# Windowed attention into a gated feed-forward block: token blocks cut 256 x4 and 512 x4, and the work of attention groups 3, 4 and 5 set at other places

## The chip, the cores and the metric

The kernel runs as one program on one core of a Trainium2 chip. The metric is the time of one execution on the device in microseconds (us), and lower is better. A core has five engines with instruction queues of their own: TensorE (PE in the profile, with its weight loads as PEld), VectorE (DVE), ScalarE (ACT), GpSimd (POOL) and SyncE (SP). They meet only through semaphores. DMAs are issued from the queues of POOL, SP and ACT; those from POOL are the profile's software queue q0, those from SP and ACT its hardware queues q1 and q10.

## The reference

```
# q, k, v: (4, 8, 768, 64) f32; n_sink = 4, window = 128
s = q @ k.T / 8
keep = (j < n_sink) or (0 <= i - j < window)       # query i, key j
a = softmax(where(keep, s, -1e9))
x = (a @ v) with the heads side by side            # 3072 tokens x 512
out = (silu(x @ w_gate) * (x @ w_val)) @ w_out     # 512 -> 1536 -> 512
```

Tokens run batch by batch: token 768*b + i is position i of batch b.

## The kernel before

**Groups and blocks.** Attention works in 12 groups of 256 tokens, three for each batch: group g is part g % 3 of batch g // 3. The feed-forward works in eight blocks of tokens, listed in `SIZES` (L42), with `OFF` as their starts. Before, block 3 is groups 3 and 4, block 4 is 5 and 6, block 5 is 7 and 8, block 6 is 9 and 10, and block 7 is group 11 alone. All matmuls are in bf16 with sums in f32.

**The steps of a group.**
- `load_nat` (L106): four POOL DMAs bring k and q of 256 tokens with tokens on partitions (the tile `nat`). From group 4 on there is one buffer for it, so the next load waits until the last has been turned. `load_v` (L143) brings the values, for the later groups of a batch (`load_vm`, L120) by three or five smaller DMAs into the tile `vm`, else by two into `va`.
- Turning k and q so that the head dimension lies on partitions (tiles `kT`, `qT`). Two ways are there: `step_TN` (L273) with 4 TensorE transposes for each of four quarters and a copy out of PSUM, or `xbar` (L287) with four DMA transposes from the queue of SP, which is called the crossbar here.
- Scores: `step_S1` (L360) issues the matmuls of all heads into six PSUM banks of the eight, `exps` the exponentials on ACT, `masks` the masking on DVE; `step_S2` and `step_S3` are the later exponentials and masks. Groups that are not the first of a batch also have the sinks' scores, `mm_K` (L422).
- Values: `step_PV` (L469), four calls for each group, with a reciprocal and a scaling on DVE that make the tile `xn`.
- `step_X` (L523): from group 3 on, one DMA transpose from SP for each 128 tokens writes `xn` into the block's `xT`, which the feed-forward reads.

**The steps of a block.** `gate` (L611) is one unit: matmuls with w_gate into `pg`, the tanh on ACT, matmuls with w_val into `pv`, two operations of DVE that write `ht`. A block of 512 tokens has 12 such units of 4 + 4 matmuls with 512 columns; a block of 256 has 6 units of 8 + 8 matmuls with 256 columns. `down` (L644) is one unit for each 128 tokens: 12 matmuls, a copy on ACT, and a DMA to the output from the queue of ACT for the early blocks and of SP for the others (L665).

**The order.** It is written out by hand. `weave` (L714) walks through a list of gate and down units and hands to unit i the attention steps that `slots` (L719) names for i. In a gate the steps lie between the two halves of the matmuls, or ahead of both where they are marked so (as `S1` is). In a down they are spread evenly over its 12 matmuls. `one(at, g)` (L687) puts the scores of g at unit `at` and the last masks one later; `pair(ga, gb)` (L873) puts two groups into a weave of 16 units.

The first weave has, before, 24 units: 0 to 11 are the gates of blocks 0 and 1, 12 to 17 the gates of block 2, 18 to 23 the downs of blocks 0, 1 and 2. In it lie groups 2, 3 and 4. Each of the next three weaves has 16 units, the 12 gates and 4 downs of a block of 512, with two groups of the next block. The last has the gates of blocks 6 and 7 and then their downs, with group 11. In block 3 the first gate is done in two halves of 256 columns (`(3, i)`), so that the second half of its tokens may arrive later.

**What orders the loads.** All loads are in one POOL queue, in program order. `behind(tb, t)` (L701) is a one-element copy on POOL that reads token t of a block's `xT`: POOL stands there until that DMA transpose has landed, and the loads after it start later. `turned(g)` (L705) does the same for `qT`. The transposes of a group by the crossbar, those of `xn` and the later output DMAs share the SP queue, again in program order. A DMA from SP or ACT takes one of eight semaphores in turn, and waits until the DMA that had it last has landed.

Of the kernel before, what the change touches and what calls it, by code (L numbers as in the profile page):

```python
# [14 lines left out]
def kernel(  # L15
# [12 lines left out]
    nc = tc.nc  # L28
    P = 128
# [9 lines left out]
    NP2 = H // 2  # L39
    GC = S // 256  # L40
    NG = B * GC
    SIZES = [256, 256, 256, 512, 512, 512, 512, 256]  # L42
    assert sum(SIZES) == NTOK and NG == 12
    OFF = [sum(SIZES[:i]) for i in range(len(SIZES))]
    PEX = (0, 1, 2)
# [34 lines left out]
    def bank(shape, dtype, name):  # L80
        return psum.tile(shape, dtype, tag="b", name=name)
# [97 lines left out]
    vcl = const.tile([P, B - 1, D + 1], FP32)  # L179
# [4 lines left out]
    one = const.tile([P, 1], FP32)  # L184
# [56 lines left out]
    def flush():  # L241
        firsts()
        for f in later:
            f()
        later.clear()
# [274 lines left out]
    def dense(t, c, n):  # L520
        return t[:, 0:c * n].rearrange("p (c n) -> p c n", c=c)

    def step_X(g, j, evict="v"):  # L523
        t0 = g * 256 + j * P
        tb = max(i for i in range(len(SIZES)) if OFF[i] <= t0)
        off = t0 - OFF[tb]
        if tb == 0 and off == 0:
            xTs["01"] = xtp.tile([P, DMC, 512], BF16, tag="xT", name="xT")
            xTs[0], xTs[1] = (xTs["01"][:, :, 256 * i:256 * (i + 1)] for i in range(2))
        elif tb > 1 and off == 0:  # L530
            xTs[tb] = dense(xtp.tile([P, DMC * 512], BF16, tag="xT", name="xT"),
                            DMC, SIZES[tb])
            if tb == 3:
                for i in range(2):
                    xTs[tb, i] = xTs[tb][:, :, 256 * i:256 * (i + 1)]
        if g not in PEX:
            def sp():
                nc.sync.dma_start_transpose(xTs[tb][:, :, off:off + P], xns[g, j])
            later.append(sp)
            return  # L540
        pt = bank([P, DMC, P], BF16, "px")
        for i in range(DMC):
            nc.tensor.transpose(pt[:, i], xns[g, j][:, i * P:(i + 1) * P], ident)  # L543

        if evict == "a":
            nc.scalar.copy(out=xTs[tb][:, :, off:off + P], in_=pt)
            return

        def dve():
            nc.vector.tensor_copy(out=xTs[tb][:, :, off:off + P], in_=pt)  # L550
        if evict == "now":
            dve()
        else:
            later.append(dve)
# [18 lines left out]
    def new_h(tb):  # L573
        if tb not in hts:
            n = SIZES[tb]
            t = hpool.tile([P, DFC * 512], BF16, tag="ht", name="ht")
# [13 lines left out]
    def gate_v(tb, f, pg, th, pv):  # L590
# [11 lines left out]
        if tb == "01":  # L602
# [4 lines left out]
        nc.vector.tensor_tensor(  # L607
            hts[tb][:, f:f + 512 // SIZES[tb]].rearrange("p a n -> p (a n)"), u, pv,
            op=ALU.mult)
# [23 lines left out]
    def gate_first(tb, f, attn):  # L633

        step_PV(1, 0, 1, "a")
        step_PV(1, 1, 1)
        flush()
        a = gate_a(tb, f)
        step_X(1, 1, "now")
        step_X(1, 0, "a")  # L640
        held.pop()()
        gate_b(tb, f, *a)

    def down(tb, ts, attn, last=False):  # L644
        at = {}
        for i, a in enumerate(attn):
            at.setdefault(DFC * (i + 1) // (len(attn) + 1), []).append(a)
        n = DFC // 4
        r0 = OFF[tb] + ts * P
        parts = [(0, 3 * P), (3 * P, DM)] if last else [(0, DM)]  # L650
        for m, (lo, hi) in enumerate(parts):
            po = bank([P, hi - lo], FP32, "pd")
            for f in range(DFC):
                for a in at.get(f, []) if m == 0 else []:
                    a()
                    flush()
                nc.tensor.matmul(  # L657
                    po, hts[tb][:, f, ts * P:(ts + 1) * P], wos[f // n][:, f % n, lo:hi],
                    start=(f == 0), stop=(f == DFC - 1))
            ot = opool.tile([P, hi - lo], FP32, tag=f"ot{hi - lo}", name="ot")  # L660
            if m == 0:
                nc.scalar.activation(ot, po, AF.Copy, scale=0.5)  # L662
            else:
                nc.vector.tensor_scalar(ot, po, 0.5, None, op0=ALU.mult)  # L664
            (nc.scalar if tb < 3 else nc.sync).dma_start(out[r0:r0 + P, lo:hi], ot)  # L665

    def gates(tb):
        return [(gate, tb, f) for f in range(0, DFC, 512 // SIZES[tb])]

    def downs(tb):  # L670
        return [(down, tb, t) for t in range(SIZES[tb] // P)]

    def A(fn, *a):
        return lambda: fn(*a)

    def TN(g, evict="av"):
        return [A(step_TN, g, i, j, evict) for j in range(2) for i in range(2)]
# [4 lines left out]
    def S1(g, apart=False):  # L682
        f = A(step_S1, g, apart)
        f.ahead = True
        return f

    def one(at, g, apart=False):  # L687
        return [(at, [S1(g, apart), A(step_S2, g, apart)]), (at + 1, [A(step_S3, g)])]

    def ahead(f):  # L690
        g = lambda: f()
        g.ahead = True
        return g

    def PVs(g):
        return [A(step_PV, g, j, hh) for hh in range(2) for j in range(2)]

    def Xs(g):
        return [A(step_X, g, j) for j in range(2)]
# [14 lines left out]
    def weave(us, slots):  # L714
        assert all(i < len(us) for i in slots)
        for i, (fn, tb, x) in enumerate(us):
            fn(tb, x, slots.get(i, []))

    def slots(*pairs):  # L719
        sl = {}  # L720
        for at, steps in pairs:
            for i, step in zip(at if isinstance(at, tuple) else (at,) * len(steps),
                               steps):
                sl.setdefault(i, []).append(step)
        return sl
# [117 lines left out]
    for f in masks1[:3]:  # L843
        f()

    g0, g1, g2 = gates(0), gates(1), gates(2)
    us = [(gate_held, *g0[0][1:]), (gate_first, *g0[1][1:]), g1[0], g1[1],
          *((gate, "01", f) for f in range(4, DFC)),
          *g2, *downs(0), *downs(1), *downs(2)]

    def L(*fs):
        def f():
            for x in fs:
                x()
        return f

    def NV(g):
        return L(A(load_nat, g), A(load_v, g))
# [2 lines left out]
        (4, TN(2)[::2]), (5, TN(2)[1::2]), ((6, 7), Ss(2)), (6, [K(2)]),  # L861
        ((8, 8), PVs(2)[:2]), (9, [A(step_PV, 2, 0, 1, "a"), A(step_PV, 2, 1, 1, "a")]),
        ((10, 11), [A(step_X, 2, 0, "a"), ahead(A(step_X, 2, 1, "a"))]),
        (11, [NV(4), lambda: nc.gpsimd.tensor_copy(out=vcl[64:128], in_=vcl[0:64])]),
        ((14, 14, 15, 15), TN(3, "aa")),
        (15, [A(xbar, 4)]), (15, [A(load_nat, 5)]), (19, [A(xbar, 5, (0,))]),
        *one(17, 3), (18, [A(step_ks, 1)]), (18, [A(step_vsb, 1)]),
        ((19, 19, 19, 20), PVs(3)), (19, [S1(4)]), (20, [L(A(step_S2, 4), A(step_S3, 4))]), (20, Xs(3)), (20, [A(xbar, 5, (1,))]),
        ((21, 21, 21, 22), PVs(4)), (21, Xs(4)[:1]),
        (22, [Xs(4)[1], flush, A(behind, 3, 511), A(load_v, 5), A(load_nat, 6)]),  # L870
        (23, [A(xbar, 6), A(turned, 6), A(load_v, 6), NV(7)])))

    def pair(ga, gb, at=0):  # L873
        return [*one(at, ga), ((4, 4, 5, 5), PVs(ga)), ((7, 7), Xs(ga)), *one(8, gb, True),
                ((12, 12, 13, 13), PVs(gb)), ((13, 13), Xs(gb))]

    weave([(gate, (3, i), 0) for i in range(2)] + gates(3)[2:] + downs(3), slots(
        (15, [A(step_ks, 2), A(step_vsb, 2)]), *pair(5, 6), (9, [flush, A(xbar, 7)]),
        (13, [flush, A(behind, 4, 511), NV(8)]),
        (15, [A(xbar, 8)]), (15, [NV(9)])))  # L880
    weave(gates(4) + downs(4), slots(
        *pair(7, 8), (3, [A(xbar, 9)]), (15, [A(step_ks, 3), A(step_vsb, 3)]),
        (3, [A(load_nat, 10)]), (13, [flush, A(behind, 5, 511), A(load_v, 10), NV(11)]),
        (15, [A(xbar, 10)])))
    weave(gates(5) + downs(5), slots(*pair(9, 10), (6, [A(xbar, 11)])))
    us = gates(6) + gates(7) + downs(6) + downs(7)
    us[-1] = (lambda tb, t, a: down(tb, t, a, True), *us[-1][1:])
    weave(us, slots(
        *one(0, 11), ((4, 4, 5, 5), PVs(11)), ((8, 9), Xs(11))))


# [33 lines left out]
```

## Time and profile before

| what | value |
|---|---|
| median of 3 runs | 234.45 us (233.47 to 234.68) |
| the profiled execution: its time, its span | 233.82 us, 231.9 us |
| granted TensorE clock, mean over the span | 0.993 |
| PE busy | 225.6 us, 97% of the span |
| DVE, ACT, POOL busy | 150.9, 106.4, 84.3 us |
| software DMA queue q0 | 79904 packets, 80.7% of 16 engines' span |
| hardware DMA queue q1 | 30672 packets, 26.7% |
| chain that ended last | PE 94% of the span |

The span runs from the first instruction to the last; the 1.9 us beside it lie outside the instructions. A matmul's end is modelled, so that a row of matmuls begins a little before the previous one's shown end; the step from one start to the next is the time that it took. A DMA share over 1 means that packets of several DMAs are open at once on an engine.

### The profile page before, as it was taken

The page shows a single profiled execution, that of the slowest core. Times are in us where ns is not written, and L with a number is a line of the kernel's source. Part 1 is how long each engine was busy: PE and PEld are TensorE (multiplying, and loading weights), DVE is VectorE, ACT ScalarE, POOL GpSimd, SP SyncE. Part 2 cuts the span into 40 slices and gives each one's busy share as a digit, 9 for nine tenths or more (in the row PEclk, how much of TensorE's full clock was granted, in tenths as well). Part 3 has the DMA queues.
Part 4 walks back from the last instruction along what each step waited for, and adds up shares of the span by engine and source line. Part 5 has one row for each costly group of instructions (what it writes and reads, how often), then busy time and mean ns, then how long its engine had stood idle before and what let it go on. Part 6 is the DMA issues. An engine that isn't in the chain of part 4 may idle for free.

```text
span 231.9 us, 5433 instructions
## 1 busy us (share of the span) xinstructions
PE 225.6 (97%) x2155; PEld 125.4 (54%) x2155; DVE 150.9 (65%) x327; ACT 106.4 (46%) x212; POOL 84.3 (36%) x123
## 2 busy tenths in 40 slices
PE   7699999999999999999999999999999999999994
PEld 3469645796555644455444454454454544487443
DVE  5878888767660797960797970597960599778000
ACT  4784486566543726423635512835612823333221
POOL 8996874960500907806353415135000000000000
PEclk9979999999999999999999999999999999999999
DMA  8999999999998998998989996989915102000132
GB/s 147 150 185 179 179 198 206 164 156 122 123 154 230 103 134 99 151 195 141 146 119 139 128 124 138 105 109 144 117 40 144 45 3 42 3 3 0 64 120 90
DMA packets 112008, 28.04 MB, mean 121 GB/s; under 512 B 99056, under 2 KB 109040, under 8 KB 111984
## 3 DMA queue, kind: packets, MB, share of 16 engines
q0 software_dynamic: 79904, 14.29, 80.7%
q1 hardware_dynamic: 30672, 11.58, 26.7%
q10 hardware_dynamic: 1408, 1.84, 2.5%
q8 instruction: 17, 0.28, 0.5%
q14 instruction: 7, 0.06, 0.1%
HBM read 29.13 MB, written 6.29 MB: 153 GB/s over the span
## 4 chain that ended last, share of the span: by engine, by line
PE 94%; DMA 2%; POOL 2%; DVE 0%; issue 0%; POOLq 0%
PE pg L564 27%; PE pv L564 27%; PE pd L657 27%; PE o L494 4%; PE s L382 3%; DMA rows<-in_q_dram 2%; PE s L326 1%; PE o L463 1%; PE pk L432 1%; PE pn L279 1%; PE o L454 1%; POOL rows L102 1%; POOL x L216 1%; PE px L543 1%; DVE xT L550 0%
## 5 line engine op out<-in xcount | busy, mean ns | idle before, releaser
L592 DVE SCALAR_TENSOR_TENSOR u<-th,pg 128x512 bf16<-128x512 f32 x72 | 49.2, 683 | 45.4 <-ACT th L584 45.1
L564 PE MATMUL pg<-xT,wg 128*128 128x512 bf16 (+1 forms) x360 | 74.2, 337 | 0.3 <-DVE xT L550 0.3
L564 PE MATMUL pv<-xT,wv 128*128 128x512 bf16 (+1 forms) x360 | 74.1, 336 | 0.0
L584 ACT ACTIVATE th<-pg 128x512 f32<-128x512 f32 x72 | 43.7, 608 | 59.6 <-PE pg L564 59.6
L657 PE MATMUL pd<-wo,ht 128*128 128x512 bf16 (+2 forms) x300 | 65.9, 370 | 0.0
L564 PEld LDWEIGHTS <-wg 128*128 128x128 bf16 x360 | 34.4, 98 | 26.7 <-issue 0.7
L564 PEld LDWEIGHTS <-wv 128*128 128x128 bf16 x360 | 33.9, 98 | 23.5 <-issue 0.2
L607 DVE TENSOR_TENSOR ht<-u,pv 128x512 bf16<-128x512 bf16 x62 | 42.5, 686 | 4.7 <-PE pv L564 0.4
L657 PEld LDWEIGHTS <-ht 128*128 128x128 bf16 x300 | 27.5, 98 | 28.4
L662 ACT ACTIVATE ot<-pd 128x512 f32<-128x512 f32 (+1 forms) x24 | 14.3, 595 | 50.2 <-PE pd L657 46.8
L395 ACT ACTIVATE e<-s 128x512 bf16<-128x512 f32 x54 | 28.5, 614 | 5.8 <-PE s L382 4.9
L113 POOL DMA_DIRECT2D nat<-in_k_dram x20 | 17.7, 895 | 29.3 <-DMA qT<-nat 27.8
L511 DVE TENSOR_TENSOR xn<-o,rcp 128x256 bf16<-128x256 f32 x45 | 17.9, 419 | 0.7
L128 POOL DMA_DIRECT2D vm<-in_v_dram x24 | 17.8, 770 | 1.2 <-DMA va<-in_v_dram 0.7
L113 POOL DMA_DIRECT2D nat<-in_q_dram x20 | 17.8, 906 | 1.0 <-DMA wv<-in_moe_w_val_dram 0.5
L494 PEld LDWEIGHTS <-e 128*128 128x128 bf16 x256 | 12.0, 100 | 6.3 <-issue 0.3
L404 DVE TENSOR_TENSOR e<-e,maskq 128x768 bf16<-128x768 bf16 x24 | 13.1, 553 | 1.9 <-ACT e L395 1.9
L151 POOL DMA_DIRECT2D va<-in_v_dram x12 | 10.7, 917 | 4.3 <-DMA wo<-in_moe_w_out_dram 2.4
L703 POOL CAST warmed<-xT 1x1 f32<-1x1 bf16 x3 | 0.5, 175 | 30.2 <-DMA xT<-xn 30.2
L503 DVE RECIPROCAL rcp<-o 128x4 f32<-128x4 f32 x48 | 7.3, 172 | 5.5 <-PE o L494 5.3
L664 DVE TENSOR_SCALAR ot<-pd 128x128 f32<-128x128 f32 x1 | 0.3, 292 | 14.3 <-PE pd L657 14.3
L333 ACT ACTIVATE e<-s 128x512 bf16<-128x512 f32 x16 | 8.3, 607 | 0.6 <-PE s L326 0.5
(86 smaller groups left out, 138.7 us busy)
## 6 DMA issues: line engine op xcount, KB each, us to landing
out_dram<-ot SPq DMA_DIRECT2D x17, 256.0 KB
nat<-in_k_dram POOLq DMA_DIRECT2D x20, 128.0 KB, 4.7
nat<-in_q_dram POOLq DMA_DIRECT2D x20, 128.0 KB, 4.9
va<-in_v_dram POOLq DMA_DIRECT2D x12, 128.0 KB, 5.9
wg<-in_moe_w_gate_dram POOLq DMA_DIRECT2D x6, 256.0 KB, 7.6
wv<-in_moe_w_val_dram POOLq DMA_DIRECT2D x6, 256.0 KB, 8.2
wo<-in_moe_w_out_dram POOLq DMA_DIRECT2D x4, 384.0 KB, 11.1
out_dram<-ot ACTq DMA_DIRECT2D x6, 256.0 KB
```

What stands on the lines that cost most here:

```text
L113: nc.gpsimd.dma_start(x[:, i, j].rearrange("p (h d) -> p h d", d=D), src[b, :, t0:t0 + P].rearrange("h p d -> p h d"))
L128: nc.gpsimd.dma_start(vms[b][p0:p1, t - 1, :, 0:D], v[b, :, t0:t0 + p1 - p0].rearrange("h p d -> p h d"))
L395: nc.scalar.activation(e_t[g][:, e0:e0 + 512], pss[g][w, i], AF.Exp, scale=scale)
L404: nc.vector.tensor_tensor(e, e, m.broadcast_to([P, 2, 384]), op=ALU.mult)
L494: nc.tensor.matmul(o, l, r, start=(c == 0 and i == 0), stop=(i == len(mms) - 1), skip_group_check=True)
L511: nc.vector.tensor_tensor(xn, po[:, :, 0:D], rcp.broadcast_to([P, 4, D]), op=ALU.mult)
L564: nc.tensor.matmul(ps[:, i * n:(i + 1) * n], ws[fi][:, c, fo * P:(fo + 1) * P], xTs[tb][:, c], start=(c == 0), stop=(c == DMC - 1))
L584: nc.scalar.activation(th, pg, AF.Tanh, scale=0.5)
L592: nc.vector.scalar_tensor_tensor(u, th, 1.0, pg, op0=ALU.add, op1=ALU.mult)
L607: nc.vector.tensor_tensor(hts[tb][:, f:f + 512 // SIZES[tb]].rearrange("p a n -> p (a n)"), u, pv, op=ALU.mult)
L657: nc.tensor.matmul(po, hts[tb][:, f, ts * P:(ts + 1) * P], wos[f // n][:, f % n, lo:hi], start=(f == 0), stop=(f == DFC - 1))
L662: nc.scalar.activation(ot, po, AF.Copy, scale=0.5)
```

## The change

`SIZES` is 256 four times and then 512 four times. Block 3 is group 3 alone, block 4 is groups 4 and 5, block 5 is 6 and 7, block 6 is 8 and 9, block 7 is 10 and 11. The first weave grows to 32 units: 24 to 29 are the gates of block 3, 30 and 31 its downs. Group 3 is turned by the crossbar (`xbar` at 12) where four calls of `TN` stood at 14 and 15. The scores of group 3 move from gate 17 to down 19, those of group 4 from down 19 to down 22, and group 5 joins this weave, with its scores at gate 28 and its values in downs 30 and 31. The loads of group 4 are issued values first. The three weaves of 16 units that follow take groups 6 and 7, 8 and 9, 10 and 11; their loads and `xbar` calls stand at other units, with `behind` at other tokens and without `turned`. In block 4 the first three gates, not only the first, are done in halves. The last weave has the 12 gates and 4 downs of block 7 and no attention.

```diff
-    SIZES = [256, 256, 256, 512, 512, 512, 512, 256]
+    SIZES = [256, 256, 256, 256, 512, 512, 512, 512]
...
-            if tb == 3:
+            if tb == 4:
                 for i in range(2):
                     xTs[tb, i] = xTs[tb][:, :, 256 * i:256 * (i + 1)]
...
-            (nc.scalar if tb < 3 else nc.sync).dma_start(out[r0:r0 + P, lo:hi], ot)
+            (nc.scalar if tb < 4 else nc.sync).dma_start(out[r0:r0 + P, lo:hi], ot)
...
-          *g2, *downs(0), *downs(1), *downs(2)]
+          *g2, *downs(0), *downs(1), *downs(2), *gates(3), *downs(3)]
...
-        (11, [NV(4), lambda: nc.gpsimd.tensor_copy(out=vcl[64:128], in_=vcl[0:64])]),
-        ((14, 14, 15, 15), TN(3, "aa")),
-        (15, [A(xbar, 4)]), (15, [A(load_nat, 5)]), (19, [A(xbar, 5, (0,))]),
-        *one(17, 3), (18, [A(step_ks, 1)]), (18, [A(step_vsb, 1)]),
-        ((19, 19, 19, 20), PVs(3)), (19, [S1(4)]), (20, [L(A(step_S2, 4), A(step_S3, 4))]), (20, Xs(3)), (20, [A(xbar, 5, (1,))]),
-        ((21, 21, 21, 22), PVs(4)), (21, Xs(4)[:1]),
-        (22, [Xs(4)[1], flush, A(behind, 3, 511), A(load_v, 5), A(load_nat, 6)]),
-        (23, [A(xbar, 6), A(turned, 6), A(load_v, 6), NV(7)])))
+        (11, [A(load_v, 4), A(load_nat, 4), lambda: nc.gpsimd.tensor_copy(out=vcl[64:128], in_=vcl[0:64])]),
+        (12, [A(xbar, 3)]), (15, [A(xbar, 4), A(load_nat, 5)]),
+        (19, [S1(3), A(step_S2, 3)]), (20, [L(A(step_S3, 3), A(step_ks, 1), A(step_vsb, 1))]),
+        ((21,) * 4, PVs(3)),
+        (22, [*Xs(3), L(A(xbar, 5), A(behind, 3, 255), A(load_v, 5)), S1(4)]),
+        (23, [L(A(step_S2, 4), A(step_S3, 4), A(load_nat, 6), A(load_v, 6))]),
+        ((25, 25, 26, 26), PVs(4)), ((27, 28), Xs(4)),
+        *one(28, 5), (29, [A(xbar, 6)]), ((30, 30, 31, 31), PVs(5)),
+        (31, [*Xs(5), L(A(load_nat, 7), A(behind, 4, 511), A(load_v, 7),
+                      A(step_ks, 2), A(step_vsb, 2))])))
...
-    weave([(gate, (3, i), 0) for i in range(2)] + gates(3)[2:] + downs(3), slots(
-        (15, [A(step_ks, 2), A(step_vsb, 2)]), *pair(5, 6), (9, [flush, A(xbar, 7)]),
-        (13, [flush, A(behind, 4, 511), NV(8)]),
-        (15, [A(xbar, 8)]), (15, [NV(9)])))
-    weave(gates(4) + downs(4), slots(
-        *pair(7, 8), (3, [A(xbar, 9)]), (15, [A(step_ks, 3), A(step_vsb, 3)]),
-        (3, [A(load_nat, 10)]), (13, [flush, A(behind, 5, 511), A(load_v, 10), NV(11)]),
-        (15, [A(xbar, 10)])))
-    weave(gates(5) + downs(5), slots(*pair(9, 10), (6, [A(xbar, 11)])))
-    us = gates(6) + gates(7) + downs(6) + downs(7)
+    weave([(gate, (4, i), f) for i in range(2) for f in (0, 2, 4)] + gates(4)[6:] + downs(4), slots(
+        *pair(6, 7), (2, [A(xbar, 7)]),
+        (7, [flush, A(behind, 5, 255), NV(8)]), (9, [A(xbar, 8)]),
+        (13, [flush, A(behind, 5, 511), NV(9)]), (15, [A(xbar, 9)])))
+    weave(gates(5) + downs(5), slots(
+        *pair(8, 9), (3, [A(load_nat, 10)]), (6, [A(xbar, 10)]),
+        (13, [flush, A(behind, 6, 511), A(load_v, 10), NV(11)]),
+        (14, [A(step_ks, 3), A(step_vsb, 3)]), (15, [A(xbar, 11)])))
+    weave(gates(6) + downs(6), slots(*pair(10, 11)))
+    us = gates(7) + downs(7)
     us[-1] = (lambda tb, t, a: down(tb, t, a, True), *us[-1][1:])
-    weave(us, slots(
-        *one(0, 11), ((4, 4, 5, 5), PVs(11)), ((8, 9), Xs(11))))
+    weave(us, {})
```

## The prediction

> **What bounds the kernel now.** I read the page's engine and slice rows first, then the chain that ended last.
>
> ```profile
> PE 225.6 (97%) x2155; PEld 125.4 (54%) x2155; DVE 150.9 (65%) x327; ACT 106.4 (46%) x212; POOL 84.3 (36%) x123
> PE   7699999999999999999999999999999999999994
> DMA  8999999999998998998989996989915102000132
> PE 94%; DMA 2%; POOL 2%; DVE 0%; issue 0%; POOLq 0%
> ```
>
> TensorE is busy from the third slice to the last but one, and the chain is nearly all its own. In the waits of PE alone there are four lines, and these are the last two: after the start the largest is 0.3 us.
>
> ```profile
> PE pt L262 <- DMA rows<-in_q_dram: 1.1, 2, 0.8
> PE pg L564 <- DVE xT L550: 0.3, 1, 0.3
> ```
>
> So the change can win only what it takes out of TensorE's stream, and loses whatever wait it brings in. Next the same chain in order of time (start, length, what), around the part that changes:
>
> ```profile
> 47.25 0.45 PE pn L279 x8
> ...
> 49.44 0.45 PE pn L279 x8
> ...
> 52.51 0.77 PE s L382 x18
> 53.28 0.98 PE pg L564 x8
> 54.26 0.87 PE pv L564 x8
> 55.13 3.45 PE pd L657 x16
> ```
>
> The two `pn` rows are the TensorE transposes of group 3, and the four rows from 52.51 on begin where the one before ends: no idle time is hidden there.
>
> **What leaves and enters TensorE's stream.** The 16 transposes go: 0.45 + 0.45 = 0.90 us. Their four copies on ACT (0.59 us each) go too and free nothing, since ACT waits 59.6 us in all for `pg`. The split of block 4's first gates makes six units of 256 columns where two stood; the chain gives 0.87 + 0.87 us for a unit of 8 + 8 and 0.86 + 0.86 for 4 + 4, so four more cost 4 x 0.02 = 0.08 us. There are four blocks of 256 before and after, so the other gates and all downs cost the same. Scores cost the same in a gate as in a down: 0.77 us, and 0.11 more in the matmuls that follow (0.98 for 0.87). Values of a sink group take 1.20 us in two gates (82.72 to 83.67 and 85.39 to 85.64) and about 1.1 us in downs; groups 4 and 5 change places, so nothing is left. At the end, downs follow directly on gates; that is so already at 168.30 us, where `pd` starts with no gap. The last down and its output are unchanged. Sum: -0.90 + 0.08 = -0.82 us.
>
> The built program's order shows that the transposes are gone and the four DMA transposes are on SP, so the rival that the change does not do what it says falls away.
>
> **The wait that is added.** The scores of group 3 must now wait for four DMA transposes. When are they asked for? Unit 18 started at 55.13; without the `pn` rows and without scores in unit 17 it starts at 55.13 - 0.90 - 0.88 = 53.35, and the scores come after 16 matmuls of the downs (3.45 us): at 56.8 us. Behind them on PE stands everything else; on ACT, the output DMA of down 18 shares a semaphore with one of these transposes, and the exponentials stand behind it, but that is the same lateness, counted once.
>
> When do the transposes land? SP finishes issuing the small `vcl` loads at 43.54 and then waits 2.1 us for them, so group 3's first can start near 45.6. How long four take, from first issue to landing, is read from two timelines: SP's start of the group, and the time at which POOL, waiting for `qT`, goes on (time, length, what, idle before and its releaser).
>
> ```profile
> 49.81 2.59 SPq L293 DMA_TRANSPOSE kT<-nat  x2
> ...
> 81.85 2.50 SPq L293 DMA_TRANSPOSE kT<-nat  x2
> ...
> 143.20 2.61 SPq L293 DMA_TRANSPOSE kT<-nat  x2
> ```
>
> ```profile
> 57.48 1.75 POOL L113 DMA_DIRECT2D nat<-in_k_dram  x2 [6.13 <-DMA qT<-nat]
> ...
> 88.31 0.17 POOL L709 CAST warmed<-qT 1x1 f32<-1x1 bf16 x1 [6.71 <-DMA qT<-nat]
> ...
> 154.36 1.76 POOL L113 DMA_DIRECT2D nat<-in_k_dram  x2 [8.41 <-DMA qT<-nat]
> ```
>
> The pairs give 7.7, 6.5 and 11.2 us. The middle one ran while loads were ending, the last beside the five value DMAs of group 10 (issued 142.13 to 145.95). Group 3's four would run beside the tail of its own values, the five value DMAs of group 4 (42.45 to about 46.3, now first) and then four `nat` DMAs. Low end 6.5: landed at 52.1, room 4.7 us. High end: 11.2, and for the `nat` DMAs behind the values four times 0.89 us more, 14.8: landed at 60.4, a wait of 3.6 us. I take 10, nearer the row beside values: landed at 55.6, room 1.2 us, no wait. A gain below nothing is excluded, since TensorE waits for no data there now.
>
> The Trainium skill (Advanced Engine Details and Errata, section X-Bar Transpose) says that transpose DMAs are as fast as regular ones and expects 350 to 400 GB/s; four of 128 KB would then move in an estimated 1.5 us, and the transposes would land soon after SP has issued them. The rows say 6.5 to 11.2 us, and I go by them. A rule that speaks against the change (DMA: Bandwidth & Descriptors, section Issuing engines are not separate DMA queues) says that DMAs of SP and POOL interleave on the same 16 engines, which is the direction of the 11.2 us row.
>
> **The later places.** Waiting behind group 3's transposes on SP are group 4's and then group 3's `xT`. On POOL, group 4's `nat` comes 3.9 us later than before, behind the values; group 5's load waits until group 4 is turned, near 46.3 + 7.4 (landing of `nat` in that stretch) + 7.7 = 61. Group 4's scores are asked for in down 22, near 67: room 6.
> - Block 3's gates start after six downs (2.59 each), two scores (0.88, 1.16) and 0.76 of values: 53.35 + 15.54 + 2.80 = 71.7. `xn` is ready near 64.7; two transposes beside group 5's `nat` take half of 7.7 to 11.2, so `xT` lands at 68.6 to 70.3. Room 1.4 to 3.1.
> - Block 4 starts at 71.7 + 6 x 1.75 + 1.2 + 1.16 + 5.18 + 1.1 = 90.8. A `nat` load and its turning have taken 10.3 to 12.1 us (78.05 to 88.31, 118.54 to 130.62). Group 5's turning, behind `xT` of group 3, lands near 76, so group 6 is turned by 88.1, and its scores are asked for at 90.8. Room 2.7.
> - The second half of block 4 is needed at 90.8 + 0.88 + 3 x 1.75 = 96.9. `xn` of group 5 is ready near 89.7, and its `xT` runs beside group 7's `nat`: landed at 93.6 to 95.3. Room 1.6 to 3.3.
> - Group 7, turned by 88.1 + 12.1 = 100.2 or a few us later beside values, is asked for near 106.4. Groups 8 to 11 have 3 us and more by the same sums.
>
> These are narrow but positive. A wait of 1 us in the first place moves all later deadlines by as much, so waits do not add up; the largest counts.
>
> **Forecast.** -0.82 us and no wait that matters. The profiled execution would go from 233.82 to 233.0; it lies 0.63 under the median of the runs, so on the scale of the median 234.45 - 0.82 = 233.6. A measurement of this kernel tells about 0.5% from no change, 1.2 us (233.3 to 235.6).
>
> **Rivals.**
> 1. Short waits. One of the rooms of 1 to 3 us is used up, because transposes beside loads vary by 4.7 us, and TensorE stands 0.4 to 2 us: 234.0 to 235.6. For it: three places have rooms under 2 us. Against it: the same kind of wait occurs nowhere before.
> 2. Slower: the crossbar starves beside the loads at group 3. From a landing after 58.8 (2 us of wait, 13.2 us for the four) the change is slower; at the high end of 14.8 us it is 234.45 - 0.82 + 3.6 = 237.2. For it: no row before has nine load DMAs queued beside four transposes. Against it: group 4's own turning met the same value loads and took 7.7.
>    In the trace TensorE's clock is 0.57 between 11 and 15 us, after the wait for `rows` (5.42 us). The skill (TensorE: Matmul & The Clock Gate, section What's actually happening) halves the clock after an idle window of about 3.4 us; a wait as long as the high end would by that rule cost an estimated 1.7 us more, which is not in the number above.
> 3. More than the transposes is won, 233.0 or less: only if the switches between scores or values and gates cost more than the rows show; I found no row for it.
>
> **How the numbers follow.** Forecast 0.52, rival 1 0.22, rival 2 0.20, rival 3 0.06. Runs of before spread over 1.2 us, so about 0.07 of the forecast can measure below 233.3: faster 0.13. Of rival 1, 0.04 ends above 235.6: slower 0.24, same 0.63. The range: its low end is the forecast less 0.7 for that spread, 232.9, and its high end takes in rival 1 and the shorter half of rival 2, to 236.2.
>
> **What would show it.** Right: no `pn` rows for group 3; the chain of waits of PE still has nothing after 20 us; six downs from near 53.4 with scores in down 19 directly after `pd`; block 3's gates near 71.7, block 4's near 90.8; the end 0.8 us earlier. Wrong: an idle time of PE, or of PEld, before L382 near 57 us that ends on a DMA of `qT` or `kT`; the same before `pg` near 72 or 97 on `xT`; a hole in DVE where group 3's masks should be.

## The result, and the profile after

| what | before | after |
|---|---|---|
| median of the runs made together (6 each) | 234.02 us (233.35 to 234.68) | 236.99 us (236.35 to 238.75) |
| ratio of the runs, 95% interval | | 1.0138 [1.0098, 1.0178] |
| profiled execution: time, span | 233.82, 231.9 us | 237.61, 235.8 us |

The change makes the kernel 1.4% slower. Here and below, the ratios leave out runs that are over 1.5% above the fastest of their kernel, which the medians keep, and they are not quotients of two medians. The forecast of 233.6 us, and its range to 236.2, lie below it.

The page after, in the rows of before: busy times, the slices of PE and DMA, and the chain that ended last.

```profile
PE 224.7 (95%) x2171; PEld 127.3 (54%) x2171; DVE 152.4 (65%) x327; ACT 104.8 (44%) x208; POOL 84.9 (36%) x124
PE   7789999997999988899999999999999999999994
DMA  8999999999699799999795989405994006200022
PE 62%; DMA 21%; POOL 11%; SPq 3%; issue 2%; DVE 0%; POOLq 0%
```

PE's busy time fell by 0.9 us, so the work did leave. But its row has holes in the tenth slice (53 to 59 us) and in slices 15 to 17 (82 to 100 us), and the chain, 94% PE before, is 32% DMA and POOL. The waits of PE name what it stood for (engine, line, releaser; total, times, longest):

```profile
PE s L382 <- DMA qT<-nat: 3.2, 2, 1.7
...
PE o L463 <- DVE e L404: 0.8, 1, 0.8
```

PE's timeline gives their places (start, length, engine, line, what; in brackets the idle time ahead and its releaser):

```profile
52.81 3.62 PE L657 MATMUL pd<-wo,ht 128*128 128x512 bf16 x16
58.12 0.84 PE L382 MATMUL s<-qT,kT 64*128 64x256 bf16 x18 [1.70 <-DMA qT<-nat]
...
88.40 0.29 PE L463 MATMUL o<-vm,e 64*64 64x65 bf16 x12 [0.84 <-DVE e L404]
...
95.10 0.84 PE L382 MATMUL s<-qT,kT 64*128 64x256 bf16 x18 [1.51 <-DMA qT<-nat]
```

The scores of group 3 in down 19 wait 1.70 us for the crossbar; the values of group 5 wait 0.84 us for group 5's masks; the scores of group 6, ahead of block 4's gates, wait 1.51 us for the crossbar again. Together 4.05 us, less the 0.82 that left: +3.2 us, where the profiled executions differ by 3.79. The rest lies in the modelled ends of matmuls: from start to start the first gap is 58.12 - 52.81 - 3.45 = 1.86 us, not 1.70, and the three make about 4.7, which gives +3.9. Nothing else in the stream grew: from the start of unit 12 to the end of the last matmul it is 186.24 us before and 190.12 after, +3.88.

This is not the clock: five of the six runs after have a mean granted clock of 0.999 or 1.0. The sixth, 238.75 us, has 0.991.

The SP queue shows when group 3 was turned, and POOL's timeline when the one `nat` buffer came free for groups 5, 6 and 7.

```profile
46.40 2.60 SPq L293 DMA_TRANSPOSE kT<-nat  x2
49.09 2.59 SPq L293 DMA_TRANSPOSE qT<-nat  x2
...
83.66 4.28 SPq L293 DMA_TRANSPOSE kT<-nat  x2
```

```profile
61.76 1.75 POOL L113 DMA_DIRECT2D nat<-in_k_dram  x2 [10.17 <-DMA qT<-nat]
...
79.31 1.77 POOL L113 DMA_DIRECT2D nat<-in_k_dram  x2 [5.60 <-DMA qT<-nat]
...
95.52 1.76 POOL L113 DMA_DIRECT2D nat<-in_k_dram  x2 [10.95 <-DMA qT<-nat]
```

Group 3's four transposes took from 46.40 to 57.98 (the landing in the chain in order of time): 11.6 us. Group 6's load starts at 79.31 and its last transpose lands at 94.97: 15.7 us for load and turning. The chain in order of time (start, length, what) joins the two places: the first wait holds up group 3's `xT`, behind which group 5's transposes stand on SP, and group 6's load waits for these.

```profile
58.12 0.84 PE s L382 x18
...
66.74 0.62 SPq L538
...
72.76 5.99 DMA qT<-nat
...
79.31 2.61 POOL nat L113 x3
81.92 7.92 DMA nat<-in_q_dram
89.85 5.11 DMA qT<-nat
```

### The profile page after: what moved, and what is told of

Its sections match the earlier page's. It is cut to its first block, busy times and chain, and to the rows that moved or that the text cites. A ratio compares the mean times of both kernels' runs of the same rounds, so it can differ in the third digit from the quotient of the medians.

```text
span 235.8 us, 5476 instructions
## 1 busy us (share of the span) xinstructions
PE 224.7 (95%) x2171; PEld 127.3 (54%) x2171; DVE 152.4 (65%) x327; ACT 104.8 (44%) x208; POOL 84.9 (36%) x124
## 4 chain that ended last, share of the span: by engine, by line
PE 62%; DMA 21%; POOL 11%; SPq 3%; issue 2%; DVE 0%; POOLq 0%
PE pd L657 20%; PE pg L564 18%; PE pv L564 18%; DMA qT<-nat 8%; DMA wo<-in_moe_w_out_dram 4%; DMA wv<-in_moe_w_val_dram 4%; DMA nat<-in_q_dram 3%; POOL nat L113 3%; PE s L382 2%; SPq L293 2%; PE o L494 2%; POOL va L151 2%; DMA vm<-in_v_dram 2%; POOL rows L102 1%; POOL wv L162 1%
## 5 line engine op out<-in xcount | busy, mean ns | idle before, releaser
L564 PEld LDWEIGHTS <-wg 128*128 128x128 bf16 x376 | 36.1, 98 | 26.2 <-DMA wg<-in_moe_w_gate_dram 1.4
L564 PEld LDWEIGHTS <-wv 128*128 128x128 bf16 x376 | 35.5, 98 | 22.9 <-issue 0.2
L607 DVE TENSOR_TENSOR ht<-u,pv 128x512 bf16<-128x512 bf16 x58 | 39.8, 686 | 4.8 <-PE pv L564 0.7
L395 ACT ACTIVATE e<-s 128x512 bf16<-128x512 f32 x54 | 28.4, 612 | 8.3 <-PE s L382 7.9
L494 PEld LDWEIGHTS <-e 128*128 128x128 bf16 x256 | 11.6, 98 | 5.6 <-issue 0.4
L382 PE MATMUL s<-qT,kT 64*64 64x64 bf16 (+4 forms) x366 | 7.9, 218 | 3.2 <-DMA qT<-nat 3.2
L404 DVE TENSOR_TENSOR e<-e,mask 128x768 bf16<-128x768 bf16 x12 | 6.6, 553 | 5.8 <-ACT e L395 5.8
```

Source lines behind the costliest of these rows:

```text
L395: nc.scalar.activation(e_t[g][:, e0:e0 + 512], pss[g][w, i], AF.Exp, scale=scale)
L404: nc.vector.tensor_tensor(e, e, m.broadcast_to([P, 2, 384]), op=ALU.mult)
L494: nc.tensor.matmul(o, l, r, start=(c == 0 and i == 0), stop=(i == len(mms) - 1), skip_group_check=True)
L564: nc.tensor.matmul(ps[:, i * n:(i + 1) * n], ws[fi][:, c, fo * P:(fo + 1) * P], xTs[tb][:, c], start=(c == 0), stop=(c == DMC - 1))
L607: nc.vector.tensor_tensor(hts[tb][:, f:f + 512 // SIZES[tb]].rearrange("p a n -> p (a n)"), u, pv, op=ALU.mult)
```

## Experiments

Two theories. **Capacity**: the DMA engines have next to no room between 43 and 115 us; transposes beside the software queue's loads take about twice as long as alone, and putting four more there makes whatever stands behind them late, wherever that is. **One bad place**: group 3's turning (or the masks, or the order of two loads) is late by itself, and mended, the rest holds. All changes are against the changed kernel unless another is named; each ratio is against the kernel before, on the same chip.

**1. Group 3 turned by TensorE as before, all else as changed.**

```diff
-        (12, [A(xbar, 3)]), (15, ...
+        ((14, 14, 15, 15), TN(3, "aa")), (15, ...
```

> Group 3 is turned by TensorE again, all else as changed. Theory (lateness is made at group 3's crossbar transposes, which run beside the loads, and is handed on through the one nat buffer): no wait of the scores near 57 us; group 4's transposes are no longer behind group 3's, so group 5's load starts near 59 instead of 61.8 us, and the wait of group 6's scores falls from 1.5 to under 0.5 us. Time 237.0 - 1.7 - 1.0 to 1.5 + 0.9 = 234.7 to 235.2. Rival (group 6's wait is made locally, by the loads beside its own transposes): that wait stays at 1.5 us and the time is near 236.2.

235.83 us against 233.36: 1.0103 [1.0082, 1.0124]. Both waits for `qT` are gone, that of group 6 too. PE's timeline has two left:

```profile
72.73 1.03 PE L564 MATMUL pg<-xT,wg 128*128 128x256 bf16 x8 [0.82 <-ACT ot L662]
...
88.24 0.29 PE L463 MATMUL o<-vm,e 64*64 64x65 bf16 x12 [0.84 <-DVE e L404]
```

The first is put down to an eviction, but POOL's copy that waits for group 3's `xT` goes on at 72.64 after 6.63 us: the transposes of `xn` landed then. Waits and the split gates make 0.82 + 0.84 + 0.08 = 1.74 us; the profiled executions differ by 1.85. So the crossbar at group 3 is a smaller part of the loss than its wait suggests: without it the kernel is still 1% slower, because the other moves have waits of their own. The way that I had expected isn't shown: group 5's load starts at 62.52, no earlier than in the change (61.76), and group 6's at 79.44 (79.31). Group 6's last transpose lands at 93.39, 1.6 us earlier than in the change, and its scores start at 93.52: they are just in time.

**2. The kernel before, with group 3 alone turned by the crossbar** (scores still in gate 17).

```diff
-        ((14, 14, 15, 15), TN(3, "aa")),
+        (12, [A(xbar, 3)]),
```

> The kernel before with one part of the change alone: group 3 turned by the crossbar at unit 12, its scores left at gate 17. Theory: the four transposes run beside group 4's loads and land 10 to 12 us after 46, at 56 to 58; the scores are asked for near 51.5 and wait 4.5 to 6.5 us, and where TensorE's clock is halved after it 1.7 us more; time 237.5 to 241. Rival (the transposes themselves are quick, and the wait in the changed kernel comes from its other parts): landed by 53, a wait under 1.5 us, time 233 to 234.5.

242.3 against 233.48: 1.0373 [1.0339, 1.0406]. SP issues the first transpose at 45.70, and PE stands for it:

```profile
58.04 1.46 PE L382 MATMUL s<-qT,kT 64*128 64x256 bf16 x18 [7.50 <-DMA qT<-nat]
```

The time is above the expected 237.5 to 241 us. Twelve microseconds for four transposes in the old order of loads too. The later scores of the change (about 6 us later) are what brings 7.5 down to 1.7.

**3. Group 4's loads in the old order, `nat` first.**

```diff
-        (11, [A(load_v, 4), A(load_nat, 4), lambda ...
+        (11, [A(load_nat, 4), A(load_v, 4), lambda ...
```

> Only the order of group 4's loads goes back: nat first, then the values. Theory (any loads beside the crossbar make it late): the wait of group 3's scores stays, 1 to 2.5 us; group 4 is turned 1 to 3 us earlier, group 6's wait shrinks by as much; time 235.5 to 237. Rival (the value loads, now first, are what makes group 3's transposes late): no wait near 57 us, time under 235.3.

237.5 against 233.36: 1.0176 [1.0147, 1.0204]. Group 3 still waits 1.94 us; the order of the two loads isn't the cause. Group 4 is turned only 0.4 us earlier (group 5's load starts at 61.39). Group 6 no longer waits, since TensorE comes there later: the clock fell after the first wait. Stretches of the windows view (from:to, length, busy of PE, PEld, DVE, ACT, POOL, then the granted clock, DMA share, GB/s):

```profile
56.00:59.00 3.00, 1.06 (x19) 0.60 (x18) 0.00 (x0) 0.42 (x2) 0.00 (x0) 1.00 1.46 171
59.00:62.50 3.50, 3.50 (x16) 1.23 (x11) 2.07 (x6) 2.89 (x6) 1.11 (x2) 0.52 0.44 125
62.50:66.00 3.50, 3.45 (x20) 1.65 (x20) 0.73 (x3) 1.19 (x2) 2.39 (x3) 0.99 1.28 135
```

**4. Group 4's loads only after group 3 has been turned.**

```diff
-        (11, [A(load_v, 4), A(load_nat, 4), lambda ...
-        (12, [A(xbar, 3)]), (15, ...
+        (11, [lambda ...
+        (12, [A(xbar, 3), A(turned, 3), A(load_v, 4), A(load_nat, 4)]), (15, ...
```

> Group 4's loads are issued only when group 3's transposes have landed. Theory: without loads beside them the four transposes land 6 to 8 us after their first issue near 46.4, by 54, and the scores of group 3 wait for nothing; but group 4's loads begin 10 us later, its scores are late by 1 to 2 us and group 6's by 2 to 4; time 237 to 240. Rival (group 3's transposes are late because they start late, or because TensorE, PSUM or ACT hold the scores): they still land near 58 and the wait of 1.7 us stays.

240.45 against 233.36: 1.0279 [1.0235, 1.0324]. POOL's copy that waits for `qT`, and PE's two waits behind it:

```profile
53.24 0.18 POOL L709 CAST warmed<-qT 1x1 f32<-1x1 bf16 x1 [3.60 <-DMA qT<-nat]
```

```profile
69.91 0.89 PE L382 MATMUL s<-qT,kT 64*64 64x192 bf16 x52 [2.78 <-DMA qT<-nat]
...
84.57 0.89 PE L382 MATMUL s<-qT,kT 64*64 64x192 bf16 x52 [2.02 <-DMA qT<-nat]
```

With those nine loads out of the way the four transposes take 46.76 to 53.24, 6.5 us instead of 11.6, and group 3 waits for nothing. That is the loads' price, shown. Group 4's transposes are held back as well, but they don't explain it: in the change the first of group 3's, issued at 46.40, lands at 53.12, before group 4's are issued (53.75), and takes 6.7 us where it takes 2.7 here. But the loads are late by what they were held, and groups 4 and 5 wait 2.78 and 2.02 us instead.

**5. Two `nat` buffers, so that loads needn't wait for the turning** (the last output tile gets a pool of its own, to make room).

```diff
-    natp = pool("natp", 1)
+    natp = pool("natp", 2)
...
+    olast = pool("olast", 1)
...
-            ot = opool.tile(
+            ot = (olast if last else opool).tile(
```

> Two nat buffers instead of one (the last output tiles get a pool of their own to make room). Theory (lateness is handed on through the one buffer): group 5's load starts near 51 us instead of 61.8, group 6's near 72 instead of 79; the wait of group 6's scores is gone, while more loads beside group 3's transposes make that wait 2 to 4 us; time 235.5 to 237.5. Rival (group 6's wait is local): it stays at 1.5 us and the time is 237 to 239.

236.33 against 233.36: 1.0128 [1.0111, 1.0145]. In the profile group 6's wait is gone and group 3's grew to 2.79: group 5's load now starts at 51.47, in the middle of group 3's turning. (That execution took 240.09 us, 3.8 over the median, so only its sequence is read.) No gain over the change.

**6. The same two buffers in the kernel before**, with the same pool for the last output tile.

```diff
-    natp = pool("natp", 1)
+    natp = pool("natp", 2)
...
+    olast = pool("olast", 1)
...
-            ot = opool.tile(
+            ot = (olast if last else opool).tile(
```

> The kernel before with two nat buffers alone, to tell what they bring without the change. Every theory: TensorE waits for no DMA there after the start, so nothing can be won, and more loads beside group 4's transposes may cost up to 1 us: 0.999 to 1.005.

236.76 against 233.31: 1.0117 [1.0065, 1.0168]; I had expected none. SP's and PE's timelines:

```profile
50.01 2.59 SPq L294 DMA_TRANSPOSE kT<-nat  x2
```

```profile
62.74 1.50 PE L383 MATMUL s<-qT,kT 64*64 64x192 bf16 x52 [3.22 <-DMA qT<-nat]
```

Before, group 4 was turned from 49.81 to 57.48, 7.7 us, because the next load stood behind it. Freed, that load (51.49 to 55.16) runs beside the transposes, which now land at 62.7: 12.7 us. So the single buffer, which looks like a limit, kept loads away from transposes, and this is the loads' price once more, with nothing of the change in it. Two things weaken it. Group 5's first transposes, issued at 57.27, run beside the end of group 4's. And the six runs lie from 234.30 to 237.59, with the profiled one the longest, so that the wait need not be as long in each.

**7. Group 3's `nat` and the sinks' loads ahead of w_out, and its turning at unit 8.**

```diff
-    for i in range(4):
-        load_out(i)
-    load_nat(3)
-    load_v(3)
     nc.gpsimd.memset(vcl, 0.0)
     nc.gpsimd.memset(vcl[:, :, D:D + 1], 1.0)
     load_sinks(vcl, 1, B)
+    load_nat(3)
+    for i in range(4):
+        load_out(i)
+    load_v(3)
...
-        (12, [A(xbar, 3)]), (15, ...
+        (8, [A(xbar, 3)]), (15, ...
```

> The changed kernel with group 3's nat loaded ahead of the four w_out loads, the sinks' loads ahead of both, and its crossbar call at unit 8. Theory: its transposes start near 38 and land by 50, so the scores in down 19 wait for nothing; group 4's transposes no longer queue behind them and land by 59 instead of 61.7; group 6's wait falls to 0.5 to 1.5 us (deadline 1.7 earlier, data 2 to 3 earlier); with the 1.2 us for group 5's masks and -0.8 saved the time is 234.3 to 235.5 on a before of 233.4 to 234.0. Rival (the crossbar takes DMA time from whatever runs beside it, so the lateness only moves): w_out or group 4's values late instead, no gain against the changed kernel.

236.74 against 233.48: 1.0118 [1.0064, 1.0173]. The first transposes go at 36.15 and group 3 doesn't wait, but w_out and group 4 are later, and about the same time is lost further on, with the 0.84 us for group 5's masks as in the change:

```profile
73.27 1.05 PE L564 MATMUL pg<-xT,wg 128*128 128x256 bf16 x8 [2.11 <-DMA xT<-xn]
...
95.03 0.84 PE L382 MATMUL s<-qT,kT 64*128 64x256 bf16 x18 [1.03 <-DMA qT<-nat]
```

**8. Group 5's scores one gate earlier**, for its masks.

```diff
-        *one(28, 5), (29, [A(xbar, 6)]), ...
+        *one(27, 5), (29, [A(xbar, 6)]), ...
```

> The changed kernel with the scores of group 5 one gate earlier (27 for 28). Theory (the chain of loads and crossbar transposes through the one nat buffer ends last at group 6's scores): the 0.8 us wait for group 5's masks goes, but the wait of group 6's scores grows by the same, since its data still land near 95 us; time within 0.5 us of the changed kernel, 1.012 to 1.016 of before. Rival (each wait costs its own time): 0.8 to 1.2 us faster than the changed kernel, about 1.009.

237.1 against 233.48: 1.0144 [1.0092, 1.0196]. The wait for the masks is gone, so two gates between scores and values were too few. The ratio is the expected one, but not in the expected way, since group 6's wait did not grow. The time isn't better: group 3 waits 2.20 in this profile, block 3's `xT` 1.15, group 6 0.39, and the earlier scores 0.47 for a bank that DVE holds.

**9. Experiment 7 with 8, and with group 5's k turned ahead of group 3's `xn`.**

```diff
-        ((21,) * 4, PVs(3)),
-        (22, [*Xs(3), L(A(xbar, 5), A(behind, 3, 255), A(load_v, 5)), S1(4)]),
+        (21, [A(xbar, 5, (0,))]), ((21,) * 4, PVs(3)),
+        (22, [*Xs(3), L(A(xbar, 5, (1,)), A(behind, 3, 255), A(load_v, 5)), S1(4)]),
```

> As the kernel with group 3's nat first, and besides the scores of group 5 at gate 27 and group 5's k turned before group 3's output transposes. Theory: all three waits go, TensorE keeps the 0.8 us saved: 232.7 to 233.8 on a before of 233.4 to 234.0, that is 0.995 to 1.000. Rival: group 6's wait stays at 1 us or more since the loads beside its own transposes make it: 1.003 or more.

241.02 against 233.48: 1.0328 [1.0287, 1.0369]. Two transposes more ahead of `xT` on SP, and block 3's gates wait 5.07 us for it (76.77). This place, which the prediction gave a room of 1.4 to 3.1, has no slack for a transpose.

**10. to 12. Fewer loads beside the later turnings.** In 10, group 6's values wait for its turning, as before; 11 adds the same for group 5 and its scores one gate earlier; 12 adds group 3's scores 1.3 us later in down 19.

```diff
-        (23, [L(A(step_S2, 4), A(step_S3, 4), A(load_nat, 6), A(load_v, 6))]),
+        (23, [L(A(step_S2, 4), A(step_S3, 4), A(load_nat, 6))]),
...
-        *one(28, 5), (29, [A(xbar, 6)]), ...
+        *one(28, 5), (29, [A(xbar, 6), A(turned, 6), A(load_v, 6)]), ...
# 11, as well
-        (22, [*Xs(3), L(A(xbar, 5), A(behind, 3, 255), A(load_v, 5)), S1(4)]),
+        (22, [*Xs(3), L(A(xbar, 5), A(turned, 5), A(load_v, 5)), S1(4)]),
...
+        *one(27, 5), ...
# 12, as well
-        (19, [S1(3), A(step_S2, 3)]), (20, [L(A(step_S3, 3), ...
+        (19, [L()] * 9 + [S1(3)]), (20, [A(step_S2, 3), L(A(step_S3, 3), ...
```

> The changed kernel with one thing back from the kernel before: POOL waits until group 6 is turned before it loads group 6's values. Theory, as the earlier runs have left it (transposes are late where loads run beside them, and the changed kernel lets them run beside): group 6's four transposes land about 10 us after its nat load starts instead of 15.7, near 90, and the wait of group 6's scores (1.5 us) goes; group 3's wait and the one for group 5's masks stay; ratio to before 1.006 to 1.008. Rival (the whole chain of loads is late by its length, whoever runs beside): group 6's wait stays at 1 us or more, ratio 1.012 or more.

> As the last, and group 5's values too are loaded only when group 5 is turned, and its scores come one gate earlier. Theory: the wait for group 5's masks goes and no DMA wait takes its place, group 3's wait of 1.7 to 2 us alone is left: -0.8 + 1.9 = +1.1 us, 1.003 to 1.006. Rival: another transpose is late in its place (group 3's output or group 5), 1.009 or more.

> As the last, and group 3's scores six matmuls later in down 19 (1.3 us). Theory: its transposes land near 58 whatever TensorE does, so its wait falls from 1.9 to 0.6 us; -0.8 + 0.6 = -0.2 us against before, 0.997 to 1.002. Rival (group 3's output, asked for at the same place, is next in line): a wait before block 3's gates takes back 0.5 to 1.3 us, 1.003 to 1.006.

| run | us, against 233.64 | ratio | waits of PE in the profile |
|---|---|---|---|
| 10 | 237.68 | 1.0189 [1.0128, 1.025] | group 3 0.81, masks 0.84, group 7 1.08 |
| 11 | 238.09 | 1.0189 [1.0132, 1.0246] | group 3 2.58, a PSUM bank 0.46, group 7 1.62 (put down to a bank) |
| 12 | 238.16 | 1.018 [1.0113, 1.0247] | block 3's `xT` 1.95, a PSUM bank 0.46, group 7 1.04 |

Group 6's wait goes in all three. In 11, group 7's last transpose lands at 110.87, and DVE frees the bank at 111.00, when its scores start: both are late. PE's timeline of 10 shows what came for group 6's wait:

```profile
110.43 0.89 PE L382 MATMUL s<-qT,kT 64*64 64x192 bf16 x52 [1.08 <-DMA qT<-nat]
```

Whatever is held back for one group is late for the next one. And 12 has only moved the first wait: the 1.3 us given to group 3's scores come back as a wait of 1.95 at `xT`. None of the three beats the change; group 6's load and turning still take 79.36 to 92.84 in 10, 13.5 us, more than the 10.3 of before. In 10 as in the change, group 4's two `xT` transposes stand just ahead on SP (from 81.19), where before they came behind (87.94), and the second transpose of k goes 3.2 us after the first (3.1 in the change), where before it went 1.3 after. That they slow group 6's load is likely, but no run takes them away.

**13. and 14. Group 3 by TensorE, on top.** 13 is 11 with `TN(3, "aa")`; 14 is the change with two `nat` buffers (and the pool of experiment 5), `TN(3, "aa")` and group 5's scores at gate 27.

```diff
-        (12, [A(xbar, 3)]), (15, ...
+        ((14, 14, 15, 15), TN(3, "aa")), (15, ...
# 14, as well
-    natp = pool("natp", 1)
+    natp = pool("natp", 2)
...
-        *one(28, 5), ...
+        *one(27, 5), ...
```

> As the second, but group 3 turned by TensorE. Theory: no DMA wait at all; the 0.9 us of transposes are paid again, so this is the kernel before plus 0.1 us: 0.998 to 1.003. Rival (block sizes or places of groups 3 to 5 cost time by themselves): 1.006 or more.

> The changed kernel with group 3 turned by TensorE, two nat buffers, and group 5's scores one gate earlier. Theory (one chain of loads and turnings, handed on through the one nat buffer and crowded between 43 and 70 us): with group 5's load issued before 56 us nothing runs beside group 3's output transposes, and no DMA wait is left; the kernel before plus 0.08 (split gates) and 0.5 (PSUM bank of group 5's scores): 1.000 to 1.004. Rival (the DMA engines as a whole are too slow for this order, whatever the buffers): a DMA wait of 1 us or more is left somewhere before 115 us, 1.006 or more.

13: 236.34 against 233.64, 1.0089 [1.0052, 1.0126]. I had expected no DMA wait; in its profiled execution (238.42 us, 2.1 over its median) the largest wait of PE after the start is 2.37 us for block 3's `xT`, at 74.39. 14: 235.03 against 233.31, 1.0055 [1.0032, 1.0078], the best order with the new blocks that was found. The waits of PE in 14:

```profile
PE s L383 <- DMA qT<-nat: 1.0, 1, 1.0
...
PE s L383 <- DVE u L593: 0.6, 1, 0.6
...
PE pk L433 <- ACT e L396: 0.2, 1, 0.2
```

With the 0.08 of the split gates these make 1.9 us, as much as the profiled executions differ (235.70 - 233.82 = 1.88). The 1.0 is group 5, at 79.73.

**15. The same without TensorE: two buffers, group 3's and the sinks' loads early as in 7, group 5's scores at 27** (of the reordering in 7 one line is shown).

```diff
-    natp = pool("natp", 1)
+    natp = pool("natp", 2)
...
+    load_nat(3)
...
-        (12, [A(xbar, 3)]), (15, ...
+        (8, [A(xbar, 3)]), (15, ...
...
-        *one(28, 5), ...
+        *one(27, 5), ...
```

> The changed kernel with two nat buffers, group 3's nat loaded ahead of w_out and turned by the crossbar from unit 8 on, and group 5's scores one gate earlier. Theory: group 3's transposes land by 50, group 5's load is over by 66 us, and no DMA wait is left; -0.8 + 0.5 = -0.3 us: 0.996 to 1.002. Rival (the DMA engines as a whole): group 3's output or group 6 waits 1 us or more, 1.005 or more.

237.29 against 233.31: 1.0145 [1.0091, 1.0199]. In its profiled execution (235.82, 1.5 us under its median) PE waits 0.57 for group 4 and 0.97 for group 5. It differs from 14 in the early loads and in four transposes on the DMA engines in place of 0.9 us on PE, and its median is 2.3 us higher.

Each wait could be taken away, in one order or another; none of these orders took them all away. That speaks against one bad place. That the DMA engines are full is not shown, for the DMA row has lulls (6 in the 11th slice), and in the change they move nothing from 78.5 to 80.5 us, just before group 6's load, which had waited for the single buffer; shown is that loads and transposes slow each other, and that what is held back for one group is late for the next. Whether some order has neither stays open.

## Why the prediction was wrong

- **-0.90 for the transposes of TensorE: right.** No `pn` rows of group 3 are left. Down 18 starts 2.16 us earlier than before, of which 0.39 came with the start of unit 12; -1.77 remains where the working has -0.90 - 0.88. **+0.08: no row speaks against it.**
- **"I take 10, nearer the row beside values": the first step that failed.** It is 11.6 us, and SP started 0.8 later. The working's high end of 14.8 had the right direction; the row that I leaned on (7.7, group 4's own turning) was quiet because the single buffer held the next load back, as experiment 6 shows. That is the mechanism of rival 2, at half of its high end: it says slower from 2 us on, and it came to 1.7 to 1.9 us.
- **Block 3's `xT`, room 1.4 to 3.1: held, with 1.4** (POOL's copy at 71.51, the gates at 72.87), but on a deadline that the wait at group 3 had already moved. That was luck: against the working's 71.7 it would have had 0.2. In experiments 1, 7, 8, 9, 12 and 13 the same place waits 0.8 to 5.1 us.
- **"Group 6 is turned by 88.1": failed by 6.9 us.** 3.3 of it is the start (group 5 turned at 79.3, not 76), 3.6 the size: 15.7 us for load and turning where 12.1 was the upper row. The lower row, 10.3, is group 6 with `turned(6)` ahead of its values; the change takes that out, and the text counted nothing for it. Experiment 10 puts it back and gets 13.5. But the upper row, group 9, had two value DMAs beside it (122.01), as group 6 has after (82.78), so the values alone don't make the 3.6.
- **Group 5's masks: a term that was missing.** "So nothing is left" for values in downs looked at PE's cost alone; with scores at gate 28 and values in down 30 DVE is 0.84 us late (experiments 5 and 8 show it there and gone).
- **"Waits do not add up; the largest counts": wrong, and the forecast rested on it.** 1.70 + 0.84 + 1.51 do add up, to the whole loss. The sentence would hold if only the deadlines moved and the data landed where the working put them. In the change's chain the data move too, from group 3's late scores through SP's queue and the single buffer to group 6. How much of group 6's lateness comes that way is not shown: in experiment 1 group 3 waits for nothing, and group 6's load starts no earlier. Had the waits been added, the rooms of 1 to 3 us and the spread of 4.7 us in the rows would have made rival 1, by an estimate, three waits of 1 us: 233.6 + 3 = 236.6 us.
- **The clock in rival 2: misread, without effect on the number.** The 5.42 us are the length of a DMA in the chain, not a wait of TensorE. TensorE itself was busy for 2.35 of the 3.50 us before its clock fell (7.90 to 11.40 us), with waits of 0.31 and 0.78 us between.
- The rule that DMAs of all issuing engines interleave on the same 16 engines (the Trainium skill, DMA: Bandwidth & Descriptors, section Issuing engines are not separate DMA queues) was cited and then weighed too little: experiments 4 and 6, 6.5 against 11.6 and 7.7 against 12.7 us, agree with it.

## What to carry to other kernels

Before work is moved from a full TensorE to the DMA engines, look at what the DMA engines already do in that stretch, and take the duration of a transfer from a row with the same neighbours, not the nearest one in kind. Where transfers are chained by a single buffer, a wait at one place doesn't use up the later ones: data and deadline can move together, and short waits add up. And a buffer that is waited for may be the thing that keeps two kinds of transfers apart: a second one cost the kernel before 1.2% (0.65% to 1.7%).

## What the hardware showed

- Four DMA transposes of k and q took 6.5 us from first issue to landing with the loads held back (experiment 4), 7.7 beside values, and 11.6, 12.2 and 12.7 beside values and `nat` loads (after, experiments 2 and 6). Each single one landed 2.4 to 2.7 us after its issue in experiment 4, and 6.7 to 7.5 us after it in the change.
- TensorE's granted clock fell to 0.5 for about 3.4 us after waits shorter than that: after 1.94 us in experiment 3, and after 3.22 in experiment 6 (0.55 to 0.59 from 62 to 66 us). In experiment 4 it fell after 2.02 us and, in the same execution, stayed at 1.0 after 2.78. In other executions a wait of 1.70 (after), 2.11 (experiment 7), 2.20 (8) or 2.58 us (11) left it at 1.0. The Trainium skill (TensorE: Matmul & The Clock Gate, section What's actually happening) lets the clock fall after an idle window of about 3.4 us and calls the window free-running; that waits of like length differ in what follows agrees, that 1.94 us of idle time suffice does not follow from it. A wait of 2 us can so cost an estimated 1.7 more (half of the 3.4) in one execution and nothing in the next.
